# Unread matmuls moved in the opening of a fused attention and gated feed-forward kernel, and its instruction order redrawn

## The chip, the cores and the metric

The kernel runs on one core of a Trainium2 chip. The metric is the device time of one execution in microseconds (us); lower is better. The engines are TensorE (PE, whose weight loads are shown as PEld), VectorE (DVE), ScalarE (ACT), GpSimd (POOL) and SyncE (SP, which only issues DMAs here).

## The reference

```python
B, N, m, C = (4, 12416, 32, 128)          # x: B x N x C, inducing: m x C
def mab(q, kv):
    s = scale * (q @ kv.transpose(0, 2, 1))
    s = s - s.max(-1, keepdims=True)
    a = np.exp(s)
    a /= a.sum(-1, keepdims=True) + 1e-09
    return a @ kv
h = mab(I, x)                              # I: inducing, for each batch
y = mab(x, h)
# y as 49664 rows of 128; w_gate, w_val: 128 x 1536; w_out: 1536 x 128
gate = 1.0 / (1.0 + np.exp(-(y @ w_gate)))
val = y @ w_val
return (gate * val @ w_out).astype(np.float32)
```

## The kernel before

**What is computed where.** First stage, per batch: 32 inducing rows attend to the 12416 rows of x, giving h (32 x 128). Second stage: each row of x attends to the 32 rows of h. Since y = a2 @ h, the kernel never forms y: it multiplies h with w_gate and w_val once per batch (the tile hw, 32 rows deep) and computes gate and value from the attention weights a2 directly, with a contraction of 32 instead of 128. The weights a2 are laid four times over the partitions (a2r), so that up to four such matmuls use four 32-row strips of the array.

**Chunks.** The rows are cut into blocks of 512, 97 in all; 1536 hidden columns are 12 groups of 128. A chunk is one block and one group: 128 partitions x 512. For each chunk of the main stream there are a gate fill and a value fill on PE (`hidden_mm`, L1149), a tanh on ACT that reads the gate bank (L1207, sigmoid written with tanh), a product (t + 1) * v on DVE that reads the value bank (L1354), and four matmuls with w_out (`out_mm`, L1298). When a block is complete its accumulator is read out, scaled by 0.5, on ACT (L1417) or DVE (L1419), and SP sends it to memory (L1324). Tanh and product take one chunk or two neighbouring ones at once: narrow (128x512) and wide (128x1024). Seven PSUM banks (vm_ps) hold fills, one (acc) the accumulator.

**Padded fills.** A fill can also run over the whole 128 rows with weights padded by zeros (its operand is then named xT, where `make_alone` puts the padded copy, L1130 and L1133 on POOL). Such a fill shares the array with no other one, but is followed by a matmul with w_out without a change of rows.

**Side chunks.** ASIDE names blocks of which one or more chunks go another way: fill (L1252), tanh into SBUF (L1262), fill, copy of the value on ACT (L1272), and the addition and multiplication on POOL (L1264, L1274).

**What sets the order.** Everything from the first fill on is issued by one string, ORDER, read word by word; the instructions of each engine then stand in that order, and each engine runs its own in order. `g01` fills gate banks 0 and 1 and issues the tanh, `v56` fills value banks, `x` is the next product, `o8` eight matmuls with w_out, `e` and `f` an evacuation on ACT or DVE; `p` and `q` are `g` and `v` with padded fills. `k31` takes the next step of chain 31, and a capital in front of a number takes it with a bank. Chains carry all other work: first-stage scores of the next batch (`s1_score_pe`, L417; maximum L429; exponential L442; transposes into a1 by SP, L468; sums L479), the second-stage softmax (scores L670, on POOL a tree for the maximum L717 to L722, sums L739, spreading L785, and SP's transposing DMA into a2r, L796), loads of x by POOL's queue (L192), their transposes into xT by SP (L201), and `make_alone`. SKIP shifts places in the ring of 16 tanh tiles.

**The opening.** Up to about 28 us the first batch's first stage runs. Then `hw_fill` (L562) forms hw of batch 0, `keep_on(2, 0)` issues two matmuls whose results nobody reads (L371), the attention weights of the first block are turned (L1092) into a2first, and the loop starts with `g01 v56`. In `fill_value` three more unread matmuls (w_ps, L1337) follow the first value fill.

Of the kernel before, what the change touches and what calls it, by code (L numbers as in the profile page):

```python
# [10 lines left out]
F32 = mybir.dt.float32  # L11
# [7 lines left out]
P = 128  # L19
# [3 lines left out]
    3, 7, 9, 11, 12, 13, 14, 24, 24, 25, 26, 27, 32, 34, 35, 36, 38, 42, 48, 50, 51, 51, 53, 56,  # L23
    58, 59, 61, 64, 68, 70, 75, 75, 79, 79, 79, 82, 84, 86, 86, 89, 90, 91, 91, 91, 95, 95,
# [15 lines left out]
    48, 111, 174, 304, 413, 491,  # L40
# [3 lines left out]
g01v56C0k0k0g34xg1v0g34xv56xo4g10v34g56xv01xk0o4v56g34k74o8g2xv01k0o4g34g56v2xo12v34g01o8xv56g2  # L44
o8ek0xk110v34g0g12xo8g0v56xk72o4g34v12k0k73o4A1o4xxk1v56k1g34o8xv01g2k1o4g34xo4g2v56o12exv01g34
C6xg56k6k76o12v34k6o4g0B114v56xo8k114g234xv0o8xv1g56o4k83k6q0o4g34xxv21o8M114A8xek8k114v12o4v34x
xk8g65o12p0o4v12g56o8g34v0o4xv56g12xo8v34xg0o8k78v12exxg56A7k7k1o12k7v34g56g12q0xo8v56g34xxo8q01
p2xo4g56v34p2o8g01v56xxg2v34o8A2ek2k2xg12v56o16k1v34xg0g12xo8v56g0k80o8k75g12v34k1k1o8v0xg56o8
q12xek8g34xg56xA10o4v12g34o8k10xv56o8xk10g34v12o8v0xg56xo12k2v34g12o8v5g6A9xk79k77k10k9v12k9xxe
g34p0v65xo8v23B115k115k82E115k2k115k2k84o12g01v56xxo12g43C12o4v01k12g56xk2k12q34o12xA18ek2k18v56  # L50
xg1p2o8v1k18g34o8k18g56v2xo4v1k18v0g34xo8v56xC116xxk116o4g1g34v0o12v56xg21o4A11k11k11v34J116xe
k116v10k81g56xo8xv2g34o8g56v01xo4p4D3xq2xk3k3o4g56v01o4xv2g43o8xv56xg01o12C14k12ek14g34v01v6g5o8
k3k85o12k14D117xk117v45g01xo4N117q23xk117o8g45v01o4p6xxg23o4q4o4v56g01k14o4C13k13xE15k13D19xk19
k15v01C118fk15k3k3k118v34g56o12C118xv1k118xxg0o8g56v23xE16g01o12v56k3k16g23o4q0o12q12xk16ek16x
g56g34v0o12xv1g56v2xo12v34xg01xo8M119xq6C4k119k4o4g01xv34o12ek3v56g2xA17k17k17g34xv1o8C119k119v0
# [6 lines left out]
exg43v56o4k22xo8k22g12v34o4xv0g56k22o8g12xxv34xo4g56v0k111o8g12v34o12exv0g56xg34xv12o8xg0v56o8
g23xv4o8xg10v56o4g23q4o8xxv01g56k21o8q2o4xeg3g56v01o4k22o4xv43xC122k122o8v56g01xo12D122C121v4
k122xo8xk121k22g01v56o12xv4D121ev01k121g56xo4v4g23o8g56xxv01o8g43xv2xo4v01xg56o12E123v2k90k92
k123xD123v01k123g56o8v4o4exxv1xg23v0G23p5k23o4xk22q4xo4k91v23xk23g10o8g56v4o8xv01g23o8g56v4xo4
v01g23o12F28xE124k22exk28k124v01C124k124xk28v6xo12g34v21o4xv0g56o8g34v12o4F125xk125v6g0o8xv34g12
# [54 lines left out]
v23o8xg56xv01o8p4xo8v23xeg56E158v01o12xk158v23g56o4xg4o8v01g56o8g2v43o4g56o4xg2xv01o4g3v45xG158  # L121
o4ep2g3v01o16k158xg23xv45xo4v6g01o12g23v4o4xv56g01xo12v43C159xexv01g56o16k159g34v56o4xg2v0g1xo12
v56g34o4xxv0g21o8xv34o4eg56v12xxg0o12v56g34xo4v01g2o8xg3v45G159g2o8k159xg01v32o8g6v4v5g01xg2xxv3
xv6o8ev45g01v32xxxz6o48
"""


@with_exitstack
def kernel(
# [9 lines left out]
    nc = tc.nc  # L139
# [1315 lines left out]
```

## Time and profile before

| | |
|---|---|
| median of three runs | 706.15 us (705.6 to 707.27) |
| profiled execution, its own time | 708.66 us |
| its span, first to last instruction | 706.9 us |
| mean granted TensorE clock | 0.992 |
| busy share of PE, DVE, ACT, POOL | 96%, 97%, 95%, 78% |

A profile shows one execution. Lines of groups read: line, engine, operation, output<-input, shape, count, then busy us and mean ns of one, then the idle time just ahead of them and what ended it. Lines of the timeline read: start, length, engine, line, operation; the bracket holds the wait just ahead and its releaser, and neighbours of the same kind are merged under the shape of the first. Lines of windows read: from:to, length, busy us of PE, PEld, DVE, ACT and POOL with counts, then the TensorE clock granted, the DMA share and GB/s. The row PEclk of the page has one digit for each fortieth of the span, 9 for 0.9 or more.

### The profile page before, as it was taken

The page shows a single profiled execution, that of the slowest core. Times are in us where ns is not written, and L with a number is a line of the kernel's source. Part 1 is how long each engine was busy: PE and PEld are TensorE (multiplying, and loading weights), DVE is VectorE, ACT ScalarE, POOL GpSimd, SP SyncE. Part 2 cuts the span into 40 slices and gives each one's busy share as a digit, 9 for nine tenths or more (in the row PEclk, how much of TensorE's full clock was granted, in tenths as well). Part 3 has the DMA queues.
Part 4 walks back from the last instruction along what each step waited for, and adds up shares of the span by engine and source line. Part 5 has one row for each costly group of instructions (what it writes and reads, how often), then busy time and mean ns, then how long its engine had stood idle before and what let it go on. Part 6 is the DMA issues. An engine that isn't in the chain of part 4 may idle for free. (4 is left out here: it accounts for less than half of the span.)

```text
span 706.9 us, 21210 instructions
## 1 busy us (share of the span) xinstructions
PE 678.8 (96%) x8446; PEld 402.3 (57%) x8446; DVE 684.5 (97%) x781; ACT 674.9 (95%) x963; POOL 548.8 (78%) x812
## 2 busy tenths in 40 slices
PE   8899999999999999999999899999999999999997
PEld 4355556655555555655655555556565555555555
DVE  6899999999999999999999999999999999999996
ACT  4689999999999999999999999999999999999995
POOL 4577798887887879889788688887899898889310
PEclk9989999999999999999999999999999999999998
DMA  9776966535346554424455832231321220322111
GB/s 211 114 134 132 188 129 120 111 77 106 92 108 122 115 118 93 102 57 93 90 105 116 155 86 45 85 67 40 78 61 46 68 70 27 81 77 47 62 45 47
DMA packets 118179, 65.74 MB, mean 93 GB/s; under 512 B 101408, under 2 KB 102208, under 8 KB 118080
## 3 DMA queue, kind: packets, MB, share of 16 engines
q1 hardware_dynamic: 112176, 50.90, 31.0%
q0 software_dynamic: 5584, 13.34, 11.3%
q8 instruction: 66, 1.08, 0.6%
q14 instruction: 33, 0.27, 0.1%
q10 hardware_dynamic: 320, 0.15, 0.1%
HBM read 27.80 MB, written 25.43 MB: 75 GB/s over the span
## 5 line engine op out<-in xcount | busy, mean ns | idle before, releaser
L1354 DVE SCALAR_TENSOR_TENSOR u<-t,vm_ps 128x1024 f16<-128x1024 f16 (+1 forms) x675 | 648.7, 1030 | 5.2 <-PE vm_ps L1149 2.3
L1207 ACT ACTIVATE t<-vm_ps 128x1024 f16<-128x1024 f32 (+1 forms) x645 | 552.0, 940 | 7.7 <-PE vm_ps L1149 5.5
L1298 PE MATMUL acc_ps<-wo,u 128*128 128x128 f16 x4448 | 354.8, 221 | 2.3 <-ACT o L1417 0.6
L1298 PEld LDWEIGHTS <-u 128*128 128x128 f16 x4472 | 262.0, 98 | 131.7 <-issue 116.9
L1149 PE MATMUL vm_ps<-a2r,hwt 32*128 32x512 f16 (+1 forms) x2129 | 282.9, 377 | 11.5 <-DVE u L1354 6.0
L1149 PEld LDWEIGHTS <-hwt 32*128 32x128 f16 x2153 | 83.5, 91 | 115.3 <-DVE u L1354 29.8
L785 POOL TENSOR_TENSOR a2n<-e,rs 128x2048 f16<-128x2048 f16 (+3 forms) x25 | 86.8, 3474 | 5.2 <-DVE rs L757 3.5
L763 POOL TENSOR_TENSOR near<-sme,minus 128x16 f32<-128x16 f32 (+1 forms) x22 | 65.3, 2966 | 0.9
L718 POOL TENSOR_SCALAR rise<-rise 128x256 f32<-128x256 f32 (+6 forms) x110 | 51.2, 465 | 9.7
L1274 POOL TENSOR_TENSOR xn_spare<-xn_spare 128x512 f16<-128x512 f32 x28 | 35.6, 1270 | 28.1 <-ACT xn_spare L1272 19.2
L1417 ACT ACTIVATE o<-acc_ps 128x512 f32<-128x512 f32 x91 | 56.6, 622 | 0.6 <-PE acc_ps L1298 0.2
L1149 PE MATMUL vm_ps<-a2r,xT 128*128 128x512 f16 x155 | 52.5, 383 | 0.6 <-ACT t L1207 0.3
L1264 POOL TENSOR_TENSOR xn_spare<-xn_spare,minus 128x512 f32<-128x512 f16 x28 | 29.2, 1041 | 18.7 <-ACT xn_spare L1262 18.4
L719 POOL TENSOR_TENSOR top<-top,rise 128x128 f32<-128x128 f32 (+3 forms) x88 | 28.5, 323 | 7.3
L739 POOL TENSOR_TENSOR sum<-sum 128x128 f32<-128x128 f32 (+3 forms) x92 | 28.4, 309 | 7.2
L717 POOL TENSOR_TENSOR rise<-top 128x128 f32<-128x128 f32 (+3 forms) x88 | 27.3, 310 | 6.9
L739 POOL TENSOR_TENSOR sum<-e 128x256 f32<-128x256 f16 (+1 forms) x23 | 15.5, 672 | 21.1 <-ACT e L731 18.3
L1274 POOL TENSOR_TENSOR xn<-xn 128x512 f16<-128x512 f32 x18 | 22.9, 1272 | 3.5 <-ACT xn L1272 2.4
L722 POOL TENSOR_TENSOR sc<-sc,top 128x512 f32<-128x512 f32 (+1 forms) x22 | 23.9, 1087 | 1.7
L1264 POOL TENSOR_TENSOR xn<-xn,minus 128x512 f32<-128x512 f16 x18 | 18.8, 1043 | 7.0 <-ACT xn L1262 6.6
L1252 PE MATMUL vm_ps<-a2r,hwt 32*128 32x512 f16 x63 | 21.4, 382 | 0.1
L1149 PEld LDWEIGHTS <-xT 128*128 128x128 f16 x155 | 13.2, 97 | 13.1 <-issue 3.1
(172 smaller groups left out, 462.2 us busy)
## 6 DMA issues: line engine op xcount, KB each, us to landing
out_dram<-o SPq DMA_DIRECT2D x96, 256.0 KB, 2.3
xn<-in_x_dram POOLq DMA_DIRECT2D x18, 512.0 KB, 6.0
xn<-in_x_dram POOLq DMA_DIRECT2D x3, 544.0 KB, 5.4
xn<-in_x_dram POOLq DMA_DIRECT2D x3, 256.0 KB, 12.5
xn<-in_x_dram SPq DMA_DIRECT2D x1, 576.0 KB, 4.7
xn<-in_x_dram SPq DMA_DIRECT2D x1, 512.0 KB, 3.8
a2r<-a2n SPq DMA_TRANSPOSE x29, 4.4
wg<-in_moe_w_gate_dram POOLq DMA_DIRECT2D x1, 384.0 KB, 12.0
```

The source lines that it names most:

```text
L718: nc.gpsimd.tensor_scalar_max(out=r, in0=r, scalar1=0.0)
L719: nc.gpsimd.tensor_tensor(out=top[:, 0:n, 0:w], in0=near, in1=r, op=ALU.add)
L739: nc.gpsimd.tensor_tensor(out=d[:, 0:n, :], in0=src[:, :, 0:w], in1=src[:, :, w : 2 * w], op=ALU.add)
L763: nc.gpsimd.tensor_tensor(out=near[:, 0:n], in0=sme[:, 0:n], in1=minus1[:, 0:n], op=ALU.pow)
L785: eng.tensor_tensor(out=a2n[:, 0:n, :, :], in0=e.unsqueeze(2).to_broadcast((P, n, 4, m)), in1=rs.unsqueeze(2).unsqueeze(3).to_broadcast((P ...
L1149: made_mm.append(nc.tensor.matmul(out[:, col : col + nb * P], w, a2r[q, o : o + nb, :].rearrange("p j t -> p (j t)"), start=True, stop=True,))
L1207: i = on(banks, nc.scalar.activation(out=span(ring, spots), in_=g, func=AF.Tanh, scale=0.5), [x for q in old for x in product_of[q]])
L1264: nc.gpsimd.tensor_tensor(out=st["t1"], in0=st["t"], in1=minus1[:, 0:1].to_broadcast((P, 512)), op=ALU.subtract,)
L1274: nc.gpsimd.tensor_tensor(out=st["t"], in0=st["t1"], in1=st["v32"], op=ALU.mult)
L1298: mm = nc.tensor.matmul(acc[0][half][:, i, :], u[:, ts(i, P)], wo16[:, j, :], start=(i in fresh), stop=not left[ib] and not any(e[1] == ib ...
L1354: x = on(banks, nc.vector.scalar_tensor_tensor(out=u[:, 0:n, a:e], in0=t[:, :, a:e], scalar=1.0, in1=v[:, :, a:e], op0=ALU.add, op1=ALU.mu ...
L1417: evac.pop()(lambda out, in_, by: nc.scalar.mul(out=out, in_=in_, mul=by))
```

## The change

`keep_on` issues four unread matmuls instead of two. The three unread ones behind the first value fill are taken out of `fill_value`; a new word `d` issues a given number of them at any place of the order, and the new ORDER has `d3` and `d2`. ORDER is a different string from its first words to its last; ASIDE has one more entry (block 7 twice), SKIP one more.

```diff
-    3, 7, 9, 11, 12, 13, 14, 24, 24, 25, 26, 27, 32, 34, 35, 36, 38, 42, 48, 50, 51, 51, 53, 56,
+    3, 7, 7, 9, 11, 12, 13, 14, 24, 24, 25, 26, 27, 32, 34, 35, 36, 38, 42, 48, 50, 51, 51, 53,
...
-    48, 111, 174, 304, 413, 491,
+    48, 84, 110, 173, 303, 412, 490,
...
-g01v56C0k0k0k0g34xg1v0g34xv56xo4g10v34g56xv01xk0o4v56g34k74o8g2xv01k0o4g34g56v2xo12v34g01o8xv56g2
+g01k72C0k0k0g34v56d3xv0xd2g1g34v56xg10v34o4g56v01k0xo4g34v56k110o8g2xv01g34o4xxg56v2k74o8xv01g34o12
...
-    keep_on(2, 0)
+    keep_on(4, 0)
...
-        if c == 0:
-            w_ps = ps.tile([P, 512], F32, tag="acc", name="w_ps")
-            for _ in range(3):
-                nc.tensor.matmul(w_ps[:], ident[:], xT[0][:, 0:4, :], start=True, stop=True)
         value["fill"] = c + len(banks)
+
+    def keep_busy(n):
+        w_ps = ps.tile([P, 512], F32, tag="acc", name="w_ps")
+        for _ in range(n):
+            nc.tensor.matmul(w_ps[:], ident[:], xT[0][:, 0:4, :], start=True, stop=True)
...
+        elif word == "d":
+            keep_busy(int(k))
```

The words of the two strings, counted:

| | before | after |
|---|---|---|
| products, wide + narrow | 444 + 230 | 431 + 255 |
| tanhs of the main stream: one, two, three chunks | 175, 467, 3 | 185, 460, 4 |
| side chunks | 46 | 47 |
| padded fills (main and side) | 184 | 164 |
| evacuations by `e` (ACT), `f` (DVE) | 91, 5 | 92, 4 |
| unread matmuls by `keep_on`, in the loop | 2, 3 | 4, 5 |

Where instructions stand now is shown at three places. On PE, at the loop's first words: the piece of the difference with the new unread matmuls (L1339, into w_ps, reading the identity and xT of batch 0), between fills that read a2first.

```order
 L1149 LDWEIGHTS hwt
 L1149 MATMUL vm_ps<-a2first,hwt 128x512
+L1339 LDWEIGHTS ident
+L1339 MATMUL w_ps<-xT_96,ident 128x512
+L1339 LDWEIGHTS ident
+L1339 MATMUL w_ps<-xT_96,ident 128x512
+L1339 LDWEIGHTS ident
+L1339 MATMUL w_ps<-xT_96,ident 128x512
 L1149 LDWEIGHTS hwt
 L1149 MATMUL vm_ps<-a2first,hwt 128x512
```

Before, the three stood behind the first four fills and ahead of the 16 scores of L670; now the scores come ahead of them, behind the first two fills, and two more follow one fill later.

On POOL, in the opening. Before: the load of batch 1's second group (L192), then the sums (L739), the spreading (L785), the padded copies of batch 0 (L1130, L1133).

```order
L687 TENSOR_TENSOR lo<-nmx,hi 128x16
L192 DMA xn_91<-in_x_dram 128x2048
L739 TENSOR_TENSOR sum_717<-e 128x256
L739 TENSOR_TENSOR sum_719<-sum_717 128x128
L739 TENSOR_TENSOR sum_721<-sum_719 128x64
L739 TENSOR_TENSOR sum_723<-sum_721 128x32
L739 TENSOR_TENSOR sum_725<-sum_723 128x16
L745 TENSOR_SCALAR sme<-sum_725 128x16
L785 TENSOR_TENSOR a2n<-e,rs 128x2048
L1130 MEMSET xT_96 128x3072
L1133 COPY xT_96<-hwt 32x768 x4
```

After, in the same place:

```order
L687 TENSOR_TENSOR lo<-nmx,hi 128x16
L1130 MEMSET xT_96 128x3072
L1133 COPY xT_96<-hwt 32x768 x4
L192 DMA xn_91<-in_x_dram 128x2048
L739 TENSOR_TENSOR sum_847<-e 128x256
L739 TENSOR_TENSOR sum_849<-sum_847 128x128
L739 TENSOR_TENSOR sum_851<-sum_849 128x64
L739 TENSOR_TENSOR sum_853<-sum_851 128x32
L739 TENSOR_TENSOR sum_855<-sum_853 128x16
L745 TENSOR_SCALAR sme<-sum_855 128x16
L785 TENSOR_TENSOR a2n<-e,rs 128x2048
```

The padded copies moved ahead of the load and of the chain that ends in a2r.

On SP, at the transposes of batch 3 (xT_3; a1 and a2r are the transposes of the two softmaxes, out_0_dram the output). Before:

```order
L201 DMA_TRANSPOSE xT_3_7107<-xn_3_3755 128x16x128
L1324 DMA out_0_dram<-o32_7135 128x512
L796 DMA_TRANSPOSE a2r_7250<-a2n_7146 128x16x128
L201 DMA_TRANSPOSE xT_3_7107<-xn_3_3755 128x16x128 x3
L1324 DMA out_0_dram<-o32_7248 128x512
L468 DMA_TRANSPOSE a1_7336<-a1T_7303 128x4x128
```

After:

```order
L201 DMA_TRANSPOSE xT_3_7009<-xn_3_3787 128x16x128 x2
L1324 DMA out_0_dram<-o32_7008 128x512
L1324 DMA out_0_dram<-o32_7170 128x512
L201 DMA_TRANSPOSE xT_3_7009<-xn_3_3787 128x16x128
L796 DMA_TRANSPOSE a2r_7288<-a2n_7049 128x16x128
L1324 DMA out_0_dram<-o32_7272 128x512
L468 DMA_TRANSPOSE a1_7383<-a1T_7343 128x4x128
```

Of the four that stood ahead of the a1 row before, one and then three (groups 0, then 2, 1 and 4), two now come first (groups 0 and 1) and one more ahead of the a2r.

More of the change, by code (lines that the diff above doesn't have):

```diff
@@ L62 @@
[L62 to L66, printed above, removed]
-xo12xF30G125ek30k28k125v01k23v4g23xo20k30xg6v23g01o8g5g6v4xo4v23g01xo8v45g6k30k93xo4k94g23xv01o4
@@ L122 @@
[L122 to L124 removed]
+g01k72C0k0k0g34v56d3xv0xd2g1g34v56xg10v34o4g56v01k0xo4g34v56k110o8g2xv01g34o4xxg56v2k74o8xv01g34o12
+v56g2k73o8xxeg0v34g12o8v56g0o4xg34v12o8A1k1k0k1g34xxv56k0o8g2xv01o4xg34o4k0k83g2v56o12v01xeg34C6
+o4xg56o8k1k6v34A114k114k6o12v56xg10xo4v2g34o8xv01g56o4g23v4o4xk76o4F8xk8ek6A114k8k114v6xv12xg43
```

152 lines of the change are left out of this document (79 added, 73 removed).

## The prediction

> **What bounds the kernel now.** I read the page's busy shares first, then the clock line, then the groups by form, then windows, then the timeline at the places where an engine waited.
>
> ```profile
> span 706.9 us, 21210 instructions
> PE 678.8 (96%) x8446; PEld 402.3 (57%) x8446; DVE 684.5 (97%) x781; ACT 674.9 (95%) x963; POOL 548.8 (78%) x812
> PEclk9989999999999999999999999999999999999998
> 41.00:690.00 649.00, 631.95 (x7846) 374.09 (x7847) 643.74 (x694) 642.43 (x906) 528.06 (x767) 1.00 0.41 90
> L1354 DVE SCALAR_TENSOR_TENSOR u<-t,vm_ps 128x1024 f16<-128x1024 f16 x443 | 519.5, 1213 | 4.2 <-PE vm_ps L1149 2.2 <-DVE u L1354 0.2
> L1354 DVE SCALAR_TENSOR_TENSOR u<-t,vm_ps 128x512 f16<-128x512 f16 x230 | 152.8, 679 | 1.0 <-ACT t L1207 0.3 <-PE vm_ps L1149 0.2 <-issue 0.2
> ```
>
> The fourth line is the steady part of the loop (41 to 690 us; the columns behind the length are busy PE, PEld, DVE, ACT, POOL, then the clock). DVE, which makes the products of L1354, is busy 643.7 of 649 us; ACT is next with 642.4. Which of the two binds is told by the spacing of instructions that follow without a wait, for a row's duration overlaps the next one's start. Two rows of DVE give it. The order has nine wide products (two chunks) in the first row, and one wide and four narrow (one chunk) in the second, which prints the shape of its first only.
>
> ```profile
> 41.42 10.27 DVE L1354 SCALAR_TENSOR_TENSOR u<-t,vm_ps 128x1024 f16<-128x1024 f16 x9 [0.33 <-PE vm_ps L1149]
> 208.10 3.60 DVE L1354 SCALAR_TENSOR_TENSOR u<-t,vm_ps 128x1024 f16<-128x1024 f16 x5
> ```
>
> Wide: (10.27 - 1.21) / 8 = 1.13 us a step. Narrow: (3.60 - 1.13 - 0.68) / 3 = 0.60 us. So 444 wide and 230 narrow products are 444 x 1.13 + 230 x 0.60 = 640 us of bare DVE steps, in a stretch from 31.1 to 697.9 us that also holds some 20 us of other DVE work: the products set the time, and only what DVE does or waits for counts. Its waits are few, and two places hold most. The first is the opening, where the TensorE clock falls (the window rows have the clock in the third column from the end):
>
> ```profile
> 29.53:32.95 3.42, 2.43 (x31) 1.10 (x29) 3.12 (x7) 2.77 (x4) 2.54 (x2) 1.00 0.82 158
> 32.95:36.36 3.41, 3.28 (x16) 0.94 (x14) 3.33 (x3) 2.45 (x4) 1.31 (x4) 0.50 0.63 67
> 36.36:39.77 3.41, 3.41 (x28) 1.67 (x26) 2.37 (x3) 2.21 (x3) 2.15 (x6) 0.50 0.96 192
> 39.77:43.18 3.41, 3.29 (x44) 1.90 (x39) 2.92 (x5) 3.27 (x5) 2.00 (x1) 1.00 0.00 0
> 30.49 0.69 DVE L681 TENSOR_REDUCE nmx<-vm_ps 128x16 f32<-128x512 f32 x1 [0.23 <-PE vm_ps L670]
> 31.09 5.51 DVE L1354 SCALAR_TENSOR_TENSOR u<-t,vm_ps 128x1024 f16<-128x1024 f16 x5
> 37.32 1.22 DVE L1354 SCALAR_TENSOR_TENSOR u<-t,vm_ps 128x1024 f16<-128x1024 f16 x1 [0.71 <-PE vm_ps L1149]
> 38.87 1.22 DVE L1354 SCALAR_TENSOR_TENSOR u<-t,vm_ps 128x1024 f16<-128x1024 f16 x1 [0.33 <-PE vm_ps L1149]
> 40.25 0.69 DVE L1354 SCALAR_TENSOR_TENSOR u<-t,vm_ps 128x512 f16<-128x512 f16 x1 [0.16 <-PE vm_ps L1149]
> ```
>
> For two stretches of 3.41 us the granted clock is 0.50, PE is busy all the time, and DVE waits for its fills: 0.71 + 0.33 + 0.16, and 0.33 more at 41.42 (above), 1.53 us together, beside 0.23 us ahead of the reduction at 30.49. The second place is one wait for a DMA:
>
> ```profile
> 382.65 8.47 SPq L201 DMA_TRANSPOSE xT<-xn  x3
> 391.62 0.40 PE L417 MATMUL vm_ps<-xT,indT 128*32 128x512 f16 x4 [2.06 <-DMA xT<-xn]
> 392.14 0.69 DVE L429 TENSOR_REDUCE nm<-vm_ps 128x1 f32<-128x512 f32 x1 [1.15 <-PE vm_ps L417]
> 393.26 1.85 DVE L1354 SCALAR_TENSOR_TENSOR u<-t,vm_ps 128x1024 f16<-128x1024 f16 x2 [0.43 <-PE vm_ps L1149]
> DMA to landing us min/median/max: 2.3/4.8/6.5
> ```
>
> The first-stage scores of batch 3's second group stand on PE while their transpose, the second of three issued from 382.65 on, lands at 391.6 (the last row is for the transposes into xT). PE loses 2.06 us, DVE 1.15 + 0.43 = 1.58 us. All other DVE waits between 41 and 690 us are 649 - 643.74 - 1.58 - 0.33 = 3.35 us in many small pieces.
>
> **The change, part by part.**
>
> *Products, side chunks, evacuations on DVE.* 13 wide products fewer, 25 narrow more (one chunk goes aside), one evacuation of L1419 less on DVE (0.68 us alone by its group, 0.60 as a step, like a narrow product). By steps: -13 x 1.13 + 25 x 0.60 - 0.60 = -0.3 us. By the groups' means, the upper bound: -13 x 1.213 + 25 x 0.679 - 0.68 = +0.5 us. I take -0.3, since the products stand back to back.
>
> *ACT.* 10 narrow tanhs more, 7 of two chunks fewer, one of three more; one side tanh and one side copy more; one evacuation more.
>
> ```profile
> L1207 ACT ACTIVATE t<-vm_ps 128x1024 f16<-128x1024 f32 x467 | 463.6, 1051 | 6.6 <-PE vm_ps L1149 4.7
> L1207 ACT ACTIVATE t<-vm_ps 128x512 f16<-128x512 f32 x175 | 107.1, 634 | 0.9 <-PE vm_ps L1149 0.6
> L1207 ACT ACTIVATE t<-vm_ps 128x1536 f16<-128x1536 f32 x3 | 4.6, 1549 | 0.2 <-PE vm_ps L1149 0.2
> L1417 ACT ACTIVATE o<-acc_ps 128x512 f32<-128x512 f32 x91 | 56.6, 622 | 0.6 <-PE acc_ps L1298 0.2 <-ACT t L1207 0.2
> ```
>
> By means, without the overlap, so an upper bound: 10 x 0.634 - 7 x 1.051 + 1.549 + 2 x 0.634 + 0.622 = +2.4 us. ACT has 649 - 642.4 = 6.6 us idle there, and as much again hidden in the overlap of its rows; it stays second. On the path: nothing, unless it bunches.
>
> *Padded fills.* 20 fewer on PE. A padded fill alone costs one matmul (59.69 to the next at 59.91, the rows below): 20 x 0.22 = -4.4 us of PE, whose idle time is 17 us already. Worth nothing directly; it lets fills be early.
>
> ```profile
> 59.69 0.38 PE L1149 MATMUL vm_ps<-a2r,xT 128*128 128x512 f16 x1
> 59.91 0.28 PE L1298 MATMUL acc_ps<-wo,u 128*128 128x128 f16 x2
> 26.59 0.61 PE L371 MATMUL vm_ps<-xT,ident 128*128 128x512 f16 x2
> 27.83 0.41 PE L1092 MATMUL vm_ps<-ident,xT 128*32 128x128 f16 x16 [0.63 <-DVE xT L1081]
> 31.89 0.86 PE L1149 MATMUL vm_ps<-a2first,hwt 32*128 32x512 f16 x4 [0.91 <-ACT t L1207]
> ```
>
> *The unread matmuls.* Two more at 26.6, 2 x 0.22 us, in front of PE's wait of 0.63 us: hidden. In the loop five instead of three, and later: three behind the second fill pair, two ahead of the next gate. Net 0.4 us of PE inside what is now a wait of 0.91 us at 31.89; without that cover they would delay the third tanh by 0.4 us at most, and ACT has slack. The window 29.53 to 32.95 is where PE is least busy (2.43 of 3.42 us), and the clock falls at its end. Five matmuls of 0.22 us instead of three raise that to about 2.9, near the 2.59 of 3.41 to 2.67 that the two windows ahead of it have without a fall behind them:
>
> ```profile
> 22.71:26.12 3.41, 2.67 (x44) 1.61 (x43) 2.59 (x11) 0.29 (x1) 1.06 (x1) 1.00 0.46 47
> 26.12:29.53 3.41, 2.59 (x39) 0.94 (x35) 2.15 (x8) 2.25 (x6) 0.99 (x3) 1.00 0.95 90
> ```
>
> So I expect the clock to hold. The sixteen scores now stand ahead of the unread matmuls, so the reduction at 30.49 also loses its 0.23 us. Bounds: from 0 to 1.53 + 0.23 = 1.76 us; I take -1.4, without the 0.33 at 41.42, which came after the clock was back.
>
> The Trainium skill, page TensorE: Matmul & The Clock Gate, Part 1 and "Why this matters for your kernels", gives a free-running window of 3413 ns, which the 3.41 us steps here agree with, and lets the clock drop for want of work only when PE idles for about 3 us or more. The trace disagrees on the second point: PE's longest wait ahead of the fall was 0.91 us. By that rule the fall here had another cause and unread matmuls would not keep it away; that is the second rival below.
>
> *The order around the 391 us wait.* Batch 3's first two transposes now leave SP together, with two output transfers and an a2r behind them (the order rows), 29 chunks ahead of where the second stood (559 products' chunks done when its word comes, instead of 588); the scores stay at chunk 597. At 0.57 us a chunk that is about 16 us earlier, against a wait of 2.06: gone, -1.58 (bounds -1.6 and -1.2, if the third group's transpose, now later, is missed by a little).
>
> *Everything else that moved.* The small waits of 3.35 us are redrawn with the order. I take +0.3, one more wait like the 0.33 at 41.42; bounds -1.0 (a third of them gone with the PE time) and +1.0.
>
> Sum: -0.3 - 1.4 - 1.6 + 0.3 = -3.0 us. The profiled execution took 708.66 us (span 706.9), 2.5 above the median of the runs, 706.15; against the median the forecast is 703.1, -0.43%. Ends of its terms: -4.6 and -0.7, so 701.5 to 705.4.
>
> **The rivals.** A measurement of this kernel tells about 0.2% (1.4 us) from no change.
>
> *The clock falls all the same* (chance 0.20). The windows are free-running and the fall may come one window on; or the unread matmuls are not what counts. Then only the reduction's 0.23 us comes from the opening: -0.3 - 0.2 - 1.6 + 0.3 = -1.8, 704.3, on the edge between faster and same.
>
> *A late load takes the place of the late transpose* (0.20). On POOL, the padding of batch 0's weights (L1130, L1133) now runs ahead of the load of batch 1's second group.
>
> ```profile
> 33.74 0.59 POOL L192 DMA_DIRECT2D xn<-in_x_dram  x1
> 44.73 2.66 POOL L1130 MEMSET xT<- 128x3072 f16 x1
> 47.46 3.42 POOL L1133 COPY xT<-hwt 32x768 f16<-32x768 f16 x4
> DMA to landing us min/median/max: 5.1/6.6/14.1
> 57.20 0.40 PE L417 MATMUL vm_ps<-xT,indT 128*32 128x512 f16 x4
> ```
>
> The load is issued at 33.74 + 2.66 + 3.42 = 39.8, lands at 46.4 by the median of the loads into xn (the fourth row), and its transpose 4.8 later, 51.2, before the scores at 57.20 less the 1.6 gained, 55.6. SP stands at that transpose, with an output transfer and the second group's a2r behind it. From a landing time of 11 us on PE waits; at the worst, 14.1, for 3.1 us, of which DVE would lose three quarters (1.58 of 2.06 above), 2.3, and a second wait at the a2r as much again at most: 705.4 to 707.7, middle 706.5: no change. For it speaks that three queues meet there; against it that DMA was idle at 40 to 43 us (the share in the row of 39.77 is 0.00).
>
> *Half clock inside the loop: slower* (0.10). Twenty full-height matmuls are replaced by 32-row ones. Each fall of two windows cost DVE 1.53 us at the opening; from the third new one on the forecast is on the other side (-3.0 + 3 x 1.53 = +1.6), with four 709.2. Against it: the clock is 1.00 from 41 to 690, with PE busy 97%.
>
> *The forecast itself*: 0.50, own range 701.6 to 704.7.
>
> **How the numbers follow.** Faster by over 0.2% (below 704.7): 0.50 x 0.93 + 0.20 x 0.6 = 0.58. Slower (above 707.6): 0.10 + 0.02 of the late load = 0.12. Same: the other 0.30. The range runs from 701.6 (low end of the likeliest case) to 707.0, which takes in the clock rival and most of the late load and leaves out the half clock in the loop.
>
> **What would show it.** Right: clock 1.00 in the windows from 29 to 43 us, no DVE wait over 0.4 us there; no DMA wait at L417; 686 products, DVE busy within 1 us of 684.5; ACT busy up 1 to 2.5 us. Wrong: clock 0.50 anywhere between 41 and 690; PE waiting at L417 or L1149 for a DMA between 50 and 62 us; DVE waits for ACT's tanhs that add up to over 1 us.

## The result and the profile after

The changed kernel takes 701.84 us (median of 7 runs, 700.51 to 703.36) against 706.17 us for the kernel before beside it (7 runs): the ratio is 0.9927, 95% interval 0.9912 to 0.9943, which is 5.1 us less (the two medians alone lie 4.3 us apart, a ratio of 0.9939, inside the interval). A second set of runs gives 0.9925 (0.9911 to 0.9939). The forecast was -3.0 us; on its base of 706.15 us the ratio makes 701.0 us, below its low end of 701.6. The sign and two of its mechanisms hold; two fifths of the gain came from steps that it had put at nothing. The profiled execution took 702.07 us with a span of 700.3.

From the page of the kernel after: span, busy shares and clock line, then the steady stretch by the same window row as before.

```profile
span 700.3 us, 21241 instructions
PE 673.8 (96%) x8450; PEld 400.0 (57%) x8450; DVE 682.6 (97%) x792; ACT 674.0 (96%) x970; POOL 550.0 (79%) x814
PEclk9999999999999999999999999999999999999999
41.00:690.00 649.00, 632.15 (x7909) 376.19 (x7911) 645.64 (x709) 644.45 (x916) 524.93 (x770) 1.00 0.42 91
```

DVE is busy 645.64 of 649 us where it was 643.74, and does 709 instructions in it instead of 694: it is the same bound, with less waiting. The opening, by windows and by DVE's timeline:

```profile
29.50:32.91 3.41, 3.24 (x20) 0.84 (x17) 3.34 (x7) 2.60 (x4) 2.52 (x2) 1.00 0.86 160
32.91:36.32 3.41, 2.91 (x29) 1.53 (x28) 3.19 (x4) 3.19 (x5) 3.32 (x4) 1.00 0.61 99
36.32:39.74 3.42, 3.27 (x43) 1.81 (x40) 3.42 (x4) 3.42 (x5) 3.24 (x5) 1.00 0.87 163
30.14 0.63 DVE L681 TENSOR_REDUCE nmx<-vm_ps 128x16 f32<-128x512 f32 x1
30.69 3.02 DVE L1355 SCALAR_TENSOR_TENSOR u<-t,vm_ps 128x1024 f16<-128x1024 f16 x3
33.93 10.86 DVE L1355 SCALAR_TENSOR_TENSOR u<-t,vm_ps 128x1024 f16<-128x1024 f16 x10 [0.22 <-PE vm_ps L1149]
```

The clock is 1.00 in all three, the four waits of 0.71, 0.33, 0.33 and 0.16 us are gone with one of 0.22 in their place, and the first product starts 0.40 us earlier (30.69 for 31.09). The wait at 391 us is gone as well (first row below, the reduction of the same scores). But the order has a new one, which the other rows show, of SP, POOL, PE and DVE:

```profile
388.46 0.68 DVE L429 TENSOR_REDUCE nm<-vm_ps 128x1 f32<-128x512 f32 x1
208.34 8.89 SPq L201 DMA_TRANSPOSE xT<-xn  x3
211.31 3.61 POOL L785 TENSOR_TENSOR a2n<-e,rs 128x2048 f16<-128x2048 f16 x1
217.33 1.71 SPq L796 DMA_TRANSPOSE a2r<-a2n  x1
223.69 0.37 PE L1149 MATMUL vm_ps<-a2r,hwt 32*128 32x512 f16 x1 [1.04 <-DMA a2r<-a2n]
225.90 5.21 DVE L1355 SCALAR_TENSOR_TENSOR u<-t,vm_ps 128x1024 f16<-128x1024 f16 x5 [1.33 <-PE vm_ps L1149]
```

The weights a2n are ready at 214.9 (211.31 + 3.61), but three transposes into xT stand ahead in SP's queue until 217.2, and DVE loses 1.33 us. Last, the tail, by the weight loads of the 48 output matmuls behind the last fills; the first row is before, the second after:

```profile
698.25 4.46 PEld L1298 LDWEIGHTS <-u 128*128 128x128 f16 x48
693.18 2.91 PEld L1298 LDWEIGHTS <-u 128*128 128x128 f16 x48
```

Before, the clock was at half from 698.5 to 702 us, and the same 48 matmuls took 1.55 us longer.

**The account.** From the first product to the end of the last one before takes 669.7 us (31.09 to 700.78), after 665.0 (30.69 to 695.72). The bare steps in it (443 wide at 1.13, 230 narrow at 0.60, other DVE work 17.5; after 430, 255 and 16.8) make 656.0 and 655.7. So waiting, small and large, fell from 13.7 to 9.4 us: -1.5 in the opening, -1.75 at 391 us, +1.4 at 225.9, and -2.4 in pieces of less than half a microsecond. With the earlier start (-0.4), the bare steps (-0.3) and the tail (-1.5) that is the span's -6.6 us. It is more than the 5.1 of the ratio because the profiled run of before took 708.66 us, 2.5 above the median, with three whole windows at half clock in its span.

**Clock windows, run by run.** Each run comes with its mean clock. One window of 3.41 us at half clock takes 0.5 x 3.41 / 705 = 0.0024 off it, so (1 - clock) x 2 x time / 3.41 counts a run's half windows. The 195 runs of this study fit one line each with a common slope of 1.00 us (0.93 to 1.07) for a half window; single runs scatter 0.5 us around it. At one kernel the windows fall differently from run to run: kernel after has runs at 0.994 (703.4 us) and at 1.000 (700.9). The last two columns of the table below use this line: how many half windows a run had in the mean, and what the kernel takes against before at equal clock (95% about ±0.4 to ±0.5).

| kernel | median, us | before beside it | ratio (95%) | half windows | at equal clock |
|---|---|---|---|---|---|
| before | | | 1 | 2.35 | 0 |
| after, both sets | 701.84, 701.91 | 706.17, 707.34 | 0.9927 (0.9912 to 0.9943), 0.9925 | 0.79 | -4.0 |
| before + unread matmuls | 706.24 | 706.82 | 0.9986 (0.9974 to 0.9998) | 1.28 | -0.1 |
| before + transpose | 705.85 | 706.82 | 0.9978 (0.9965 to 0.9991) | 2.18 | -1.6 |
| before + both | 703.33 | 706.82 | 0.9945 (0.9929 to 0.9960) | 0.58 | -1.7 |
| after - unread matmuls | 703.24 | 706.82 | 0.9949 (0.9929 to 0.9969) | 3.09 | -4.5 |
| after, a2r first | 705.79 | 707.34 | 0.9977 (0.9961 to 0.9993) | 2.31 | -1.6 |
| after, 23 fills twice | 703.72 | 707.34 | 0.9952 (0.9938 to 0.9966) | 0.41 | -1.7 |
| after + 2 unread | 701.23 | 707.34 | 0.9920 (0.9905 to 0.9936) | 0.25 | -3.8 |
| after, transpose earlier | 702.18 | 707.71 | 0.9918 (0.9896 to 0.9940) | 1.30 | -4.4 |
| before + both, 20 fewer padded | 702.77 | 707.71 | 0.9929 (0.9909 to 0.9948) | 0.34 | -2.7 |
| after, three edits | 700.74 | 707.71 | 0.9903 (0.9885 to 0.9921) | 0.62 | -4.7 |
| after, none padded | 707.37 | 707.71 | 0.9999 (0.9987 to 1.0012) | 2.49 | +0.1 |
| after, lone ones not padded | 706.71 | 707.78 | 0.9994 (0.9979 to 1.0010) | 1.18 | +0.7 |
| after, mixed ones not padded | 701.78 | 707.78 | 0.9919 (0.9903 to 0.9934) | 0.69 | -4.0 |
| after, mixed, + the two edits | 700.97 | 707.78 | 0.9912 (0.9895 to 0.9929) | 0.62 | -4.4 |

### The profile page after: what moved, and what is told of

The parts are those of the page before. It is cut to its first block, busy times and chain, and to the rows that moved or that the text cites. A ratio compares the mean times of both kernels' runs of the same rounds, so it can differ in the third digit from the quotient of the medians.

```text
span 700.3 us, 21241 instructions
## 1 busy us (share of the span) xinstructions
PE 673.8 (96%) x8450; PEld 400.0 (57%) x8450; DVE 682.6 (97%) x792; ACT 674.0 (96%) x970; POOL 550.0 (79%) x814
## 4 chain that ended last, share of the span: by engine, by line
PE 47%; ACT 18%; DVE 8%; issue 5%; SPq 1%; DMA 1%; DVEq 0%; ACTq 0%
PE acc_ps L1298 24%; PE vm_ps L1149 20%; ACT t L1207 14%; DVE u L1355 7%; ACT o L1420 2%; PE vm_ps L1252 1%; SPq L201 1%; DMA a2r<-a2n 1%; ACT xn_spare L1272 1%; PE vm_ps L670 0%; ACT sc L707 0%; PE vm_ps L417 0%; PE vm_ps L479 0%; ACT xn L1272 0%; PE vm_ps L1298 0%
## 5 line engine op out<-in xcount | busy, mean ns | idle before, releaser
L1207 ACT ACTIVATE t<-vm_ps 128x1024 f16<-128x1024 f32 (+2 forms) x649 | 552.2, 942 | 4.2 <-PE vm_ps L1149 2.8
L1298 PE MATMUL acc_ps<-wo,u 128*128 128x128 f16 x4444 | 351.1, 220 | 2.1 <-ACT o L1420 0.4
L1298 PEld LDWEIGHTS <-u 128*128 128x128 f16 x4468 | 259.4, 98 | 130.8 <-issue 116.9
L1149 PE MATMUL vm_ps<-a2r,hwt 32*128 32x512 f16 (+1 forms) x2149 | 287.4, 377 | 13.0 <-DVE u L1355 4.8
L785 POOL TENSOR_TENSOR a2n<-e,rs 128x2048 f16<-128x2048 f16 (+3 forms) x25 | 86.8, 3473 | 5.7 <-DVE rs L757 4.0
L1420 ACT ACTIVATE o<-acc_ps 128x512 f32<-128x512 f32 x92 | 58.2, 632 | 1.1 <-PE acc_ps L1298 0.8
L1274 POOL TENSOR_TENSOR xn_spare<-xn_spare 128x512 f16<-128x512 f32 x28 | 35.5, 1269 | 26.7 <-ACT xn_spare L1272 16.8
L1149 PE MATMUL vm_ps<-a2r,xT 128*128 128x512 f16 x133 | 45.3, 383 | 1.0 <-DVE u L1355 0.7
L739 POOL TENSOR_TENSOR sum<-sum 128x128 f32<-128x128 f32 (+3 forms) x92 | 28.3, 307 | 7.2
L739 POOL TENSOR_TENSOR sum<-e 128x256 f32<-128x256 f16 (+1 forms) x23 | 15.4, 671 | 12.1 <-ACT e L731 11.9
L1149 PEld LDWEIGHTS <-xT 128*128 128x128 f16 x133 | 11.6, 98 | 11.2 <-DVE u L1355 3.6
```

Source lines behind the costliest of these rows:

```text
L739: nc.gpsimd.tensor_tensor(out=d[:, 0:n, :], in0=src[:, :, 0:w], in1=src[:, :, w : 2 * w], op=ALU.add)
L785: eng.tensor_tensor(out=a2n[:, 0:n, :, :], in0=e.unsqueeze(2).to_broadcast((P, n, 4, m)), in1=rs.unsqueeze(2).unsqueeze(3).to_broadcast((P ...
L1149: made_mm.append(nc.tensor.matmul(out[:, col : col + nb * P], w, a2r[q, o : o + nb, :].rearrange("p j t -> p (j t)"), start=True, stop=True,))
L1207: i = on(banks, nc.scalar.activation(out=span(ring, spots), in_=g, func=AF.Tanh, scale=0.5), [x for q in old for x in product_of[q]])
L1274: nc.gpsimd.tensor_tensor(out=st["t"], in0=st["t1"], in1=st["v32"], op=ALU.mult)
L1298: mm = nc.tensor.matmul(acc[0][half][:, i, :], u[:, ts(i, P)], wo16[:, j, :], start=(i in fresh), stop=not left[ib] and not any(e[1] == ib ...
```

## The experiments

### One part at a time on the kernel before

The unread matmuls alone, at the places that after has:

```diff
-    keep_on(2, 0)
+    keep_on(4, 0)
-g01v56C0k0k0g34xg1v0g34xv56x...
+g01v56C0k0k0g34d3xg1v0d2g34xv56x...
```

> The kernel before, in its own order, with the unread matmuls of the kernel after: four instead of two ahead of the loop, three behind the second fill pair and two ahead of the next gate instead of three behind the first value fill. Theory (the unread matmuls are what keeps the clock in the opening): clock 1.00 in the windows from 29 to 43 us, the DVE waits of 0.71, 0.33, 0.33 and 0.16 us at 37 to 41 us and the 0.23 ahead of nmx gone, the wait at 391 us still there, time -1.4 to -1.9 us against before. Rival 1 (the windows are free-running and the fall comes anyway, one window on): a window of 0.50 between 33 and 45 us, time within 0.5 us of before. Rival 2 (the opening is worth more than its waits, because the phase of the windows decides the tail's clock too): clock 1.00 in the opening and also in the last 6 us, time -2.5 to -3.5 us.

Measured: -0.14% (about -1.0 us, interval -0.1 to -1.8): 1.28 half windows a run, against 2.08 in the 23 runs of before beside it and 2.35 in all 74, and nothing (-0.1) at equal clock. In the profiled run the clock fell all the same, 1.6 us later and for one window instead of two:

```profile
31.12:34.54 3.42, 2.90 (x19) 0.89 (x18) 3.42 (x4) 2.91 (x4) 3.12 (x5) 1.00 0.69 126
34.54:37.95 3.41, 3.41 (x23) 1.63 (x23) 2.63 (x3) 2.30 (x4) 1.58 (x4) 0.50 0.89 129
```

The windows of this run lie 1.6 us later than those of before's profile; the one that ends at 34.54 has PE busy for 2.90 us, and the next is granted at 0.50. Three of its eleven runs have a clock of 1.000, of the 74 runs of before none. So the theory and the first rival are both partly right: the unread matmuls act through the clock, and make a fall rarer, not impossible.

The one transpose (the step `k104` directly behind `k103`):

```diff
-...k45k103o4k45x... ...k135xG135k104C50k135...
+...k45k103k104o4k45x... ...k135xG135C50k135...
```

> The kernel before, in its own order, with one step moved: the transpose of batch 3's second group is issued directly behind that of the first, some 16 us earlier. Theory: PE's wait of 2.06 us at 391 us and DVE's 1.15 + 0.43 behind it go, everything else stays, the clock still falls in the opening; time -1.2 to -1.6 us against before. Rival (the wait is handed on to the next load or a2r in SP's queue, which now stands behind that transpose): a new DVE wait of over 1 us between 360 and 420 us, time within 0.5 us of before.

Measured: -0.22% (-1.6 us), and -1.6 at equal clock. DVE's rows at the place show no wait:

```profile
391.14 0.68 DVE L428 TENSOR_REDUCE nm<-vm_ps 128x1 f32<-128x512 f32 x1
391.74 6.95 DVE L1353 SCALAR_TENSOR_TENSOR u<-t,vm_ps 128x1024 f16<-128x1024 f16 x7
```

The theory holds, at the upper end of its range, and nothing took the wait over.

Both edits together:

```diff
-...g34xg1v0g34x... ...k103o4k45... ...G135k104C50...
+...g34d3xg1v0d2g34x... ...k103k104o4k45... ...G135C50...
```

> The kernel before, in its own order, with both edits: the unread matmuls as after has them and the one transpose moved. The products stay 443 wide and 230 narrow and 47 less one chunks stay aside. Theory A (the two named parts carry what was forecast, and the redrawn order carries the rest of what after gained): -2.8 to -3.3 us against before, clock 1.00 in the opening, no wait at 391 us; after stays 1.0 to 2.5 us faster than this kernel. Theory B (the two parts and the tail's clock are all; the redrawn order is worth nothing): within 0.7 us of after, -4.2 to -5.2 us against before. Theory C (each part alone is worth less than its waits): less than -2 us.

Measured: -0.55% (-3.9 us), 0.58 half windows, -1.7 at equal clock. Theory A holds in the main: at equal clock after is another 2.3 us (±0.5) faster, so the redrawn order is worth that much by itself. Theory B would have needed -4.2 or more, which the ratio alone doesn't exclude (its interval is -2.8 to -5.0); what speaks against it is the comparison at equal clock. "Clock 1.00 in the opening" isn't so in every run: the profiled one (706.46 us) has a half window there, from 34.09 to 37.50 us, while the other four have mean clocks of 0.999 and 1.000.

### The kernel after without its unread matmuls

```diff
-    keep_on(4, 0)
+    keep_on(2, 0)
-...g34v56d3xv0xd2g1g34v56x...
+...g34v56xv0xg1g34v56x...
```

> The kernel after without its five unread matmuls in the opening of the loop, and with two instead of four ahead of the loop; everything else as after. Theory: PE's work in the windows from 29 to 37 us sinks by 1 us, the clock falls to 0.50 for one or two windows there, DVE waits 1 to 2 us for fills, time +1.2 to +2.0 us against after (-3.0 to -4.0 against before). Rival (after's order, with its different first steps, would keep the clock by itself, or the fall comes from the phase of the windows alone): clock 1.00 from 29 to 43 us, time within 0.5 us of after (-4.7 to -5.6 against before).

Measured: 0.9949, so +0.22% (1.6 us) against after; 3.1 half windows a run instead of 0.8. At equal clock it is 0.5 us (±0.5) faster than after, which is about as much as the seven unread matmuls may cost. The clock's own windows in the profiled run, with PE's and DVE's waits:

```profile
27.82:31.23 3.41, 2.53 (x44) 1.19 (x44) 2.22 (x6) 2.89 (x5) 1.41 (x2) 1.00 0.65 89
31.23:34.64 3.41, 3.10 (x16) 0.85 (x14) 3.23 (x4) 2.40 (x4) 3.33 (x5) 0.50 0.62 125
34.64:38.06 3.42, 3.42 (x24) 1.71 (x23) 2.65 (x3) 2.63 (x3) 3.31 (x3) 0.50 0.98 181
31.14 0.55 PE L1148 MATMUL vm_ps<-a2first,hwt 32*128 32x512 f16 x2 [0.53 <-ACT t L1206]
36.95 1.22 DVE L1354 SCALAR_TENSOR_TENSOR u<-t,vm_ps 128x1024 f16<-128x1024 f16 x1 [0.77 <-PE vm_ps L1148]
```

Without the unread matmuls the clock falls for two windows, from 31.23 to 38.06 us. The theory holds, and the rival on order or phase alone falls: none of its six runs has a clock above 0.995, of after's twelve ten have.

The Trainium skill, page TensorE: Matmul & The Clock Gate, "Why this matters for your kernels", warns of idle gaps of PE of more than some 3 us, because one idle window takes the clock down. PE's longest wait here between 27 and 35 us was 0.64 us, and the clock dropped: the measurement decides, and so long a gap isn't needed. That the clock drops only behind such gaps was the prediction's own reading.

PE's busy time in the window isn't what counts either. The first row below is the kernel after, the next two a second profile of the same kernel, the last two the kernel before:

```profile
30.08:33.50 3.42, 2.75 (x15) 0.68 (x13) 3.42 (x5) 2.61 (x5) 3.04 (x4) 1.00 0.96 176
30.03:33.45 3.42, 2.76 (x14) 0.63 (x12) 3.42 (x4) 2.62 (x4) 3.21 (x5) 1.00 0.95 172
33.45:36.86 3.41, 3.41 (x23) 1.52 (x22) 2.48 (x4) 2.35 (x4) 3.34 (x3) 0.50 0.51 94
387.93:391.34 3.41, 1.63 (x25) 1.19 (x22) 3.06 (x3) 3.04 (x5) 1.64 (x2) 1.00 1.30 122
391.34:394.76 3.42, 3.14 (x40) 1.83 (x39) 2.19 (x3) 2.38 (x3) 3.00 (x6) 1.00 1.00 252
```

With 2.75 us busy the clock held, with 2.76 it fell, and with 1.63 it held. What sorts them is the work counted by the part of the array that it uses: each matmul's columns in units of 512, times its rows / 128 and its weight columns / 128, so that a 32-row fill counts a quarter and an unread or padded one a whole. A matmul across a border counts by the part inside, at 0.22 us for 512 columns (0.44 at half clock). By this count the three windows hold 6.04, 5.56 and 6.00, the one ahead of before's fall 5.69, the ones ahead of the fall in before + unread matmuls 5.47 and in this kernel 5.71. In all 17 profiles, cut into the clock's own windows from 10 us on, each of the 32 windows with half clock behind it holds less than 6.0 (19 of them lie in the tail), and of the other 3398 all but three hold 6.0 or more. This is a count over traces; no run was made to test it.

### The kernel after again, and three edits of it

> The kernel after once more, on the chip of the three kernels beside it. If the time of one run is set by how many clock windows of 3.41 us fall to half (the runs so far lie on a line of about 1 us for each, 700.9 us at a mean clock of 1.000), its runs lie on that line again: 700.5 to 701.5 at a clock of 0.999 or 1.000, 702.5 to 703.5 at 0.994. If the clock is not the reason, runs of equal clock differ as much as all of them.

Measured: 701.4 to 701.9 us at a clock of 1.000 (up to 0.4 us above what was expected), 702.1 and 702.6 at 0.997. The line holds to some 0.5 us.

The a2r ahead of the two transposes:

```diff
-...k22g56xk93k92o8q4... ...G125k22v43x...
+...k22g56xo8q4... ...G125k22k93k92v43x...
```

> The kernel after with the two transposes of batch 2 that stand in SP's queue ahead of one a2r moved behind that a2r. Theory (the a2r waits in the queue for the transposes, and PE and DVE for the a2r): the a2r is issued at 215 us instead of 217.3, DVE's wait of 1.33 us at 225.9 goes, time -1.0 to -1.4 us against after at equal clock, some -5.5 to -6.5 against before. Rival (the transposes, now later, make the first-stage scores of batch 2 wait, or the a2r takes as long for another reason): a DMA wait at L417 or still one at L1149 between 215 and 260 us, time within 0.4 us of after.

Measured: 0.9977, 2.4 us slower than after at equal clock: both the theory and its rival named the wrong sufferer.

```profile
214.83 1.92 SPq L795 DMA_TRANSPOSE a2r<-a2n  x1
216.84 5.94 SPq L200 DMA_TRANSPOSE xT<-xn  x2
227.13 2.52 SPq L467 DMA_TRANSPOSE a<-a1T  x2
229.67 0.24 PE L478 MATMUL vm_ps<-xn,a 128*32 128x128 f16 x4 [2.38 <-DMA a<-a1T]
232.32 1.82 DVE L1354 SCALAR_TENSOR_TENSOR u<-t,vm_ps 128x1024 f16<-128x1024 f16 x2 [3.73 <-PE vm_ps L1148]
```

The a2r leaves at 214.83, as worked out, and its wait is gone. But the 6 us of transposes now stand ahead of the first stage's a<-a1T (224.4 in after, 227.1 here), PE waits 2.38 us for that and more behind it, and DVE 3.73 instead of 1.33. In this profile the clock is at half from 231.05 to 234.46 us, behind a window in which PE was busy for 0.50 us, and the runs have 2.31 half windows for 0.79, which adds to the 2.4 us. Here a place in a full queue was not won but passed on.

Some value fills issued twice (a fill is one matmul of 512 columns into its bank, and the second writes the same again). The expectation counted twenty; the page has 8473 matmuls for 8450, so there were 23, or 23 x 0.22 = 5.1 us:

```diff
-            for i in hidden_mm(what, j, vm[0][:, k, :], whole):
-                on((k,), i, made_hw)
+            twice = what == "v" and not whole and 40 <= j and j % 48 == 8
+            for _ in range(1 + twice):
+                for i in hidden_mm(what, j, vm[0][:, k, :], whole):
+                    on((k,), i, made_hw)
```

> The kernel after with 20 of its 32-row value fills issued twice, one in every 48 chunks from chunk 56 on: about 20 x 0.22 = 4.4 us more on PE, as much as the 20 padded fills that the change took away; nothing else moves. Theory H1 (the small DVE waits fell by some 2.4 us because PE has this work less): 41 to 690 us has PE 3 to 5 us busier at the same progress, small DVE waits up by 1.5 to 2.5 us, time +1.5 to +2.5 us against after. Theory H2 (the small waits fell because of the order itself, which spreads wide and narrow products otherwise; PE's work is hidden either way): small waits up by less than 0.7 us, time within 0.7 us of after at equal clock.

Measured: +2.3 us at equal clock. By the account above, DVE's waiting is 11.9 us instead of 9.5 (second profile of after), nearly all in small pieces. PE's busy time rose by 2.8 us (677.6 for 674.8 in the second profile of after, both with one half window in the opening). H1 holds at its upper end: of PE's 2.8 us the time shows 2.3, though PE is busy only 97%.

Two more unread matmuls in the opening:

```diff
-...g34v56xg10v34o4g56...
+...g34v56xg10d2v34o4g56...
```

> The kernel after with two more unread matmuls, ahead of the value fill at 33.4 us where PE waits 0.50 us for a tanh. Theory (the windows are free-running, so in some runs of after one still ends where PE is idle in the opening and the next is granted at half): no half clock before 690 us in any phase, mean clock of the runs 0.998 to 1.000 instead of 0.9976, time -0.4 to -1.0 us against after in the mean, no change at equal clock. Rival (the half windows that after's runs still have lie in the tail): mean clock as after's, time within 0.3 us. Second rival (the unread matmuls stand ahead of a fill that DVE waits for): +0.3 to +0.5 us at equal clock.

Measured: 0.9920, four of five runs at 1.000, 0.25 half windows instead of 0.79; +0.2 at equal clock, within the error. It does what the theory says, but what is left to win is about half a microsecond, and five runs don't settle it.

### Making room for the a2r the other way

```diff
-...g21o8ek91v56x...
+...g21o8k91ev56x...
```

> The kernel after with one step moved: the first of the three transposes of batch 2 that stand at 208.34 us in SP's queue is issued ahead of the output transfer at 207.8 us instead of behind it, so SP does it in its idle time from 201.6 us on. Theory (it is SP's queue that delays the a2r): the other two transposes end at 214 us, the a2r is issued at 215 instead of 217.3, DVE's wait at 225.9 (0.7 to 1.4 us) goes, nothing else is late; time -0.6 to -1.4 us against after. Rival (that transpose waits for something else than the queue, such as room in xT, and holds up the output transfer and all behind it): it is issued at 205 us or later, DVE waits as before or more, time within 0.3 us of after or slower.

Timeline of SP, and DVE at the place:

```profile
200.05 4.41 SPq L200 DMA_TRANSPOSE xT<-xn  x2
208.14 0.33 SPq L1323 DMA_DIRECT2D out_dram<-o  x1
208.56 5.40 SPq L200 DMA_TRANSPOSE xT<-xn  x2
215.18 2.04 SPq L795 DMA_TRANSPOSE a2r<-a2n  x1
221.85 11.07 DVE L1354 SCALAR_TENSOR_TENSOR u<-t,vm_ps 128x512 f16<-128x512 f16 x11
```

The transpose runs in SP's idle time ahead of the output transfer, the a2r leaves at 215.2, and DVE makes eleven products past 225.9 us without a wait. The theory's mechanism holds; its size, -0.4 us (±0.5) at equal clock, is under the expected -0.6 to -1.4, and the runs don't separate it from none. The wait of 1.33 us was an unlucky draw: in the second profile of after it was about 0.6 us.

### What padding is worth

Twenty chunks' padded fills made 32-row ones in the kernel before with both edits (`p` to `g`, `q` to `v`, next to other 32-row fills):

```diff
-...g56v34p2o8g01... ...v56xg1p2o8...
+...g56v34g2o8g01... ...v56xg1g2o8...
```

> The kernel before with the unread matmuls of after and the one transpose moved (as the earlier kernel with both edits), and 20 chunks' padded fills made 32-row fills, those next to other 32-row fills, as spread over the loop as they lie; the order stays. Theory H1 (PE's work is what sets the small DVE waits): PE 3 to 4.4 us less busy, small waits down by 1.5 to 2 us, time -1.3 to -2.0 us against the kernel with both edits at equal clock, -5.0 to -5.8 against before. Rival 1 (the fill saves no time on PE, since it waits for the matmul ahead of it in its own rows): PE's busy time and the time stay within 0.5 us. Rival 2 (full-height matmuls are what keeps the clock in the loop): windows of 0.50 between 41 and 690 us, +1 us for each.

Measured: -1.0 us (±0.7) against the kernel with both edits at equal clock, less than H1's -1.3 to -2.0 but of its sign; no half window inside the loop.

The kernel after with three edits at once: the two more unread matmuls, the transpose ahead of the output transfer, and 20 more padded fills made 32-row ones:

```diff
-...xg10v34o4... ...o8ek91... ...p... ...q...
+...xg10d2v34o4... ...o8k91e... ...g... ...v...
```

> A try at a better kernel: after with two more unread matmuls at 33.4 us, the transpose issued ahead of the output transfer at 207.8 us, and 20 more chunks' padded fills made 32-row fills. If PE's work sets the small waits, the three add up: -0.3 - 0.9 - 1.6 = -2.8 us against after, 699.1 us, -1.1% against before. If only the named waits count: -1.2. If 32-row fills cost clock inside the loop: +1 us for each half window.

Measured: 0.9903, the lowest ratio of the study; -0.7 (±0.5) at equal clock against after. The parts don't add up to -2.8.

All 133 of the main stream's padded chunks as 32-row fills (every `p` is `g`, every `q` is `v`):

```diff
-...g34xo8p12xq0o4... ...v12xxp0g56...
+...g34xo8g12xv0o4... ...v12xxg0g56...
```

> The kernel after with none of the 133 chunks' padded gate and value fills padded; all are 32-row fills (the 31 side fills that are padded stay). Theory H1 to its end: PE up to 20 us less busy, DVE's small waits near nothing, time -2 to -5 us against after, until DVE's own steps or ACT bind. Rival 1 (a 32-row fill of a row group that is just in use saves nothing): PE's busy time within 3 us of after's, time within 1 us. Rival 2 (the padded fills keep the clock up): a mean clock under 0.98 and +1 us for each half window, slower than after by more than 3 us.

Measured: 0.9999: the whole gain of the change is gone, 4.1 us at equal clock, while PE's busy time stays (674.4 for 673.8 and 674.8). H1 and its first rival didn't foresee that; the second did, but by a mean clock under 0.98, and it is 0.994. The runs have 2.49 half windows for 0.79 besides, and the profile has one inside the loop, behind a window that holds 5.78 by the count above:

```profile
223.67:227.09 3.42, 2.83 (x27) 1.26 (x25) 2.85 (x4) 2.71 (x6) 3.17 (x5) 1.00 1.19 217
227.09:230.50 3.41, 3.41 (x29) 2.15 (x29) 2.54 (x3) 2.52 (x4) 2.74 (x9) 0.50 0.69 137
```

The 133 fills were then split in two, the first piece of the difference above being of the lone ones and the second of those next to 32-row fills:

```diff
-...g34xo8p12xq0o4...
+...g34xo8g12xv0o4...
```

> The kernel after with 79 of its 133 padded gate and value fills made 32-row fills: those that have no 32-row fill next to them. In the traces a lone padded fill between two runs of output matmuls takes 0.27 us from the one to the other, a lone 32-row fill 0.47. Theory (PE's lateness at the place sets DVE's small waits): some 26 lone fills cost PE 0.20 us more each, 5 us, and the time rises by half to all of that, +2.5 to +5 us against after at equal clock, all of what the kernel without padded fills lost. Rival (padding helps in another way, by the clock, wherever it stands): half of that kernel's +4 us or less, mean clock lower than after's.

```diff
-...v12xxp0g56...
+...v12xxg0g56...
```

> The kernel after with the other 54 of the 133 made 32-row fills: those next to 32-row fills, which run beside each other in other rows. Theory: up to 54 x 0.22 us less on PE where it is late, so -1 to -2.5 us against after at equal clock. Rival (padding helps wherever it stands): +1 to +2 us. Rival 2 (PE's work doesn't matter): within 0.5 us.

Measured: the lone 79 cost +4.7 us, the mixed 54 nothing (0.0 ± 0.5), together what all 133 cost. PE's busy time, from the pages of the two:

```profile
PE 678.7 (96%) x8450; PEld 396.9 (56%) x8450; DVE 685.2 (97%) x792; ACT 676.3 (96%) x970; POOL 551.1 (78%) x814
PE 670.6 (96%) x8450; PEld 398.3 (57%) x8450; DVE 682.9 (98%) x792; ACT 674.0 (96%) x970; POOL 551.0 (79%) x814
```

Against the two profiles of after (673.8 and 674.8) PE's 3.9 to 4.9 us more cost 4.7, its 3.2 to 4.2 us less bring nothing. Why a lone fill is dear without padding is in PE's timeline; the first three rows are after's, the last three those of the kernel with the lone ones not padded:

```profile
105.83 0.40 PE L1298 MATMUL acc_ps<-wo,u 128*128 128x128 f16 x4
106.06 0.38 PE L1149 MATMUL vm_ps<-a2r,xT 128*128 128x512 f16 x1
106.28 0.61 PE L1298 MATMUL acc_ps<-wo,u 128*128 128x128 f16 x8
107.18 0.40 PE L1297 MATMUL acc_ps<-wo,u 128*128 128x128 f16 x4
107.51 0.39 PE L1148 MATMUL vm_ps<-a2r,hwt 32*128 32x512 f16 x1
107.83 0.62 PE L1297 MATMUL acc_ps<-wo,u 128*128 128x128 f16 x8
```

From four output matmuls over a fill to the next ones takes 0.45 us (105.83 to 106.28) padded and 0.65 (107.18 to 107.83) in 32 rows: 0.10 us at each change of form. Over the whole profiles, a fill that stands alone takes 0.27 us in the median from the last output matmul ahead of it to the next one when it is padded (41 places in after where PE doesn't wait), and 0.47 in 32 rows (28 such places in the other kernel); two side by side take 0.49 and 0.47, so that only the 26 places that changed from the first kind to the second cost PE anything: 26 x 0.20 = 5.1 us. The Trainium skill, page TensorEngine Tiling (Array Packing), "Key Properties", says that a change of the tiling mode drains the engine; the trace agrees, and puts a price on it. The theory holds with PE's lateness at the place; its half on the mixed ones fails: PE's relief there takes nothing off after's remaining small waits.

The last one takes the mixed 54 and the two edits of the opening and of SP's queue together:

```diff
-...xg10v34o4... ...o8ek91... ...v12xxp0g56...
+...xg10d2v34o4... ...o8k91e... ...v12xxg0g56...
```

> The same 54 fills made 32-row fills, with two more unread matmuls at 33.4 us and the transpose issued ahead of the output transfer at 207.8 us. If the parts add up: -1.5 - 0.4 and fewer half windows, 699 to 700 us at the median, -1.0 to -1.2% against before; the stall at 225.9 us gone, clock 1.00 in the opening.

Measured: 0.9912, 700.97 us. It is no better than the version with three edits (their intervals overlap almost wholly); either is ahead of before by 0.9 to 1.0%, and of after by 0.1 to 0.25%, a difference that these runs don't separate from none with certainty.

## Why the prediction was right and wrong, step by step

- **Products and evacuations, -0.3:** right by count and step (430 wide and 255 narrow inside the stretch, 655.7 for 656.0 us); DVE's busy time, 682.6 for 684.5 us, fell by more than the 1 us given for it.
- **ACT, up 1 to 2.5 us and off the path:** it went down, from 674.9 to 674.0; off the path it was.
- **The unread matmuls, -1.4:** right in kind, and near in size partly by luck. The edit alone gave about -1.0, through 0.8 half windows fewer than in the runs of before beside it, at 1.00 us each; taking the unread matmuls out of after cost 1.6. What the prediction had too simply is "the clock holds": it holds in most runs, and the second profile of after has a half window at 33.45 us. Its first rival is therefore true of some single runs. Its reason, the window in which PE is least busy, is wrong: before has one with 1.63 us at 387.93 us and no fall behind it.
- **The transpose, -1.6:** right, -1.6 when made alone.
- **Half clock in the loop as rival:** not in either profile of after. Its mechanism is real: without any padded fill in the main stream one half window falls at 227.09 us. That is 3.41 of 649 us, so the mean over the stretch still rounds to 1.00.
- **The late load as rival:** the load was issued at the worked-out time (39.7 for 39.8 us), its transpose at 45.0 and the a2r at 48.7, and the scores at 53.95 us didn't wait. The new wait for an a2r is at 225.9 us instead, from SP's queue; it cost 0.4 us (±0.5) by the kernel that removes it.
- **Padded fills, "worth nothing directly", and everything else, +0.3 with a bound of -1.0:** here it failed. These terms measured -2.0 us together in place of +0.3 (the order's -2.3 at equal clock, less the products' -0.3). The reasoning was that PE's 17 us of idle time would hide 4.4 us more or less. 23 fills issued twice showed that it hides little of an addition (2.3 of 2.8 us of busy time came through), and 20 fewer padded fills in the order before brought -1.0 (±0.7). If the 20 that the change took away are worth as much, which no run shows, then with +0.4 for the a2r some -1.4 us of small waits is left that no experiment pinned to one place or mechanism; its cause stays open. The prediction also took 3.35 us of visible gaps as all that the small waits could give, while DVE's spacing beyond its bare steps held 13.7 us before.
- **The tail:** not priced. Before had half a clock there in its profile, 1.55 us on 48 matmuls. It belongs to the same lottery of windows as the opening; 1.6 half windows a run fewer, opening and tail together, make 1.6 us of the 5.1; how they divide between the two no run shows.
- **The ends of the sum:** the low end, -4.6, is added rightly. The high end is not: with the terms' own upper bounds (+0.5, 0, -1.2, +1.0) it is +0.3, not -0.7.

## What to carry to other kernels

Read the clock of every run, not of one profile: where windows fall by chance of phase, kernels are compared at equal clock, and a few unread matmuls in a thin window change a chance, and not one fixed wait. A mean of the clock over a long stretch hides a single window. PE at 97% hid little of an addition, but relief of it paid only where PE was the one that was late. A transfer that was moved within a full queue handed its wait to the next consumer; look for the queue's idle time instead.

## What the hardware showed that I had not expected

- A lone 32-row matmul between full-height ones costs 0.20 us more than the same work padded with zeros to 128 rows (0.65 for 0.45 us), 0.10 us for each change of form; two side by side cost the same either way (0.47 for 0.49). 79 fills changed to 32 rows, 26 of them alone, cost 4.7 us of 701.
- The clock fell to half for one or two windows of 3.41 us with no wait of PE over 0.91 us ahead (before). Not PE's busy time decided (held with 1.63 us, fell with 2.90), but the work weighted by the part of the array in use: in 17 profiles all 32 windows with half clock behind them hold less than 6.0 full matmuls of 512 columns, and all but three of the other 3398 hold 6.0 or more. By that count a full-height unread or padded matmul weighs as much as four 32-row fills.
- A half window costs 1.00 us here in the mean of 195 runs.
